# A third query block in two halves, and VectorE's share of the exponentials carried into the last block

## The chip, the cores and the metric

The kernel runs on one core of a Trainium2 chip. A core has five engines, each with an instruction queue of its own: TensorE (PE, matrix products into PSUM), VectorE (DVE), ScalarE (ACT, activation functions), GpSimd (POOL) and SyncE (SP, which here starts the DMAs). Each works through its queue in order and waits on semaphores where another engine's result or buffer is needed. The metric is the time of one launch on the device, in microseconds.

## What is computed

A transformer block of 2048 rows and 640 columns: layer norm, attention with 32 heads of 20 columns, output projection and residual; then layer norm, a gated layer with 1728 hidden columns, and residual. Weights and activations are bf16.

```python
def reference(A_x, A_wqkv, A_wo, B_x, B_w_gate, B_w_up, B_w_down):
    def _A_ref(x, wqkv, wo):
        ...
        scores = jnp.einsum("bhqd,bhkd->bhqk", q, k) * (Dh ** -0.5)
        p = _softmax(scores, axis=-1)
        o = jnp.einsum("bhqk,bhkd->bhqd", p, v)
        ...
    def _B_ref(x, w_gate, w_up, w_down):
        g = jnp.einsum("bsd,df->bsf", x, w_gate)
        u = jnp.einsum("bsd,df->bsf", x, w_up)
        return jnp.einsum("bsf,fd->bsd", g * u, w_down)
    x = A_x
    h = x + _A_ref(_layernorm(x, axis=-1), A_wqkv, A_wo)
    h2 = h + _B_ref(_layernorm(h, axis=-1), B_w_gate, B_w_up, B_w_down)
    return h2
```

## The kernel before

**Tiles.** The 32 heads form 8 groups of 4 (`NG`, `HPG`); a group's heads lie at 32-row slots, so the K=32 score matmuls of a group run side by side in different rows of the array. The 2048 query rows form 4 blocks of 512 (`QB`), the keys 16 tiles of 128 (`NT`). Scores stand transposed: keys on partitions, queries along the free dimension. A *segment* is one group of one query pass over all keys; the list `segs` (L303 to L311) fixes their order: block 0 (its first four groups in four key chunks, while the projections are still made), then pass "1" and pass "2" with whole blocks of 512 queries, then block 3: groups 0 and 1 whole (pass "3", `SPLIT_G` = 2), groups 2 to 7 first for the first 256 queries (pass "A") and then for the last 256 (pass "B"). Below, block means query block, counted from 0, so that the third block is block 2.

**A score tile.** The units of all segments are strung together and cut into 683 tiles of 1536 columns (`EW`, three PSUM banks; two such tiles exist). `emit_S` (L440) writes the score matmuls of a tile (L450) and then one exponential on ACT (L463) which makes the probabilities `E` in bf16; the softmax's maximum is replaced by a constant shift, and the sums come out of an extra column of ones in the values `vx`.

**A unit for VectorE.** For some tiles the last 512 columns are left to DVE. `x_takes` (L474) decides, `emit_x` (L480) writes the first pass, which reads the scores from PSUM (L488, `xv`), and queues four more: L498 (`xm`), L499 and L500 (`xt`), L493 (`xe`), which together build the bits of a bf16 exponential. ACT then does 1024 columns of that tile. The queued passes (`x_pieces`) are one queue, worked off front to back by `step_x` whenever the planner sees DVE free. In block 3 `x_takes` allows a unit only when no other work is waiting.

**Probabilities times values.** `emit_AV` (L588) takes the units whose probabilities are there in groups and accumulates them in the one bank `acc` (L619), 8 matmuls of 512 columns or 16 of 256. When a segment is full, DVE copies it to `asb` (L630), and it is normalised: by `norm` (L525), where the sums go to DRAM and back, are inverted and spread by six DMAs on SP, and POOL multiplies (L549, into `On`); or, for the segments in `FAST` (the last of a pass, on which an output projection waits), by `job_norm` (L574) with matmuls by an identity (`sums_to_rows`, L559 to L566; `rows_to_cols`, L571) and one DVE product (L582). POOL's multiplication for block b waits until the projection of block b-1 has read `On`: `("om", b - 1) in done` (L546).

**Jobs.** Between the score tiles TensorE does other work, in *jobs*: generators that yield after a matmul or at a place where the job may be left. The bank `mi` is their only accumulator. `run_job` (L429) continues a job as long as the planner's own clock (`at`, with constants such as `S_NS` and `EXP_NS`) shows room before ACT needs the next scores. `urgent` jobs go ahead of others (`step`, L365). Where there is no work, `keep_warm` (L424) puts in two filler matmuls that feed nothing (L427).

**The tail of a block.** When all groups of a block are normalised, `add_tail` (L975) queues: load the rows of x and the first weights, `job_out` (output projection and residual, L834 and L838; the layer norm's steps go to DVE's queue `aux`; then transposes, L260), `job_glu` (the gated layer, for 512 columns by `glu_sum`, L900, L247 and L908; for 256 by `glu_pair`, L918, L923 and L925; weights come in pairs of 256 hidden columns, the next pair is asked for when the one before starts, the last four pairs stay resident from the start of block 3), `job_y` (second matrix, L955, residual L959, result stored by SP, L965). So block 0's tail runs during pass "1", and so on; block 2's during block 3. Block 3's tail comes in two halves: rows 0 to 255 during pass "B", where the load and the projection are put into `urgent` if block 2's results are half out (`early`, L992), and the rest in `last_tail` (L1035) after the last exponential. One half row of the first half's `y` is held back (`some`, `held`) and placed in `last_tail`'s layer norm by `fill` (L1076).

**The loop** (L1125) goes through the tiles: scores and exponential, AV, events, a look whether a block is normalised, a job, fillers, spare DVE steps.

Of the kernel before, what the change touches and what calls it, by code (L numbers as in the profile page):

```python
# [57 lines left out]
X_LEAST, X_OUT = 3, 6  # L58
# [13 lines left out]
def kernel(  # L72
# [23 lines left out]
    ep = pool("ep", 6)  # L96
# [132 lines left out]
    def dve(ns):  # L229
        ready = at["pe"] + LAT  # L230
        spare(ready)
        at["dve"] = max(at["dve"], ready) + ns
# [69 lines left out]
    PASS = {"0": (0, 0, QB), "1": (1, 0, QB), "2": (2, 0, QB), "3": (3, 0, QB), "A": (3, 0, HW), "B": (3, HW, HW)}  # L302
# [6 lines left out]
    segs += [(p, g, 0, NT, "only") for p in "12" for g in range(NG)]  # L309
    segs += [("3", g, 0, NT, "only") for g in range(SPLIT_G)]  # L310
    segs += [(p, g, 0, NT, "only") for p in "AB" for g in range(SPLIT_G, NG)]  # L311
    FINAL = len(segs) - 1
    FAST = {("2", NG - 1), ("A", NG - 1), ("B", NG - 2)}
# [15 lines left out]
    x_pieces = deque()  # L329
    x_left = {}  # L330
    x_put = []
    x_live = {"units": 0}
    x_last = set()
# [7 lines left out]
    waiting = deque()  # L341
    aux = deque()
# [21 lines left out]

    def step():  # L365
        if cur["fresh"] and (urgent or waiting):
            if cur["gen"] is not None:
                jobs.appendleft((cur["key"], cur["gen"]))
            cur["key"], cur["gen"] = (urgent or waiting).popleft()
# [33 lines left out]
    def step_aux():  # L403
        while aux:
            try:
                at["dve"] += next(aux[0]) or 200
                return True
            except StopIteration:
                aux.popleft()
        return False  # L410

    def spare(until):
        while at["dve"] + (x_pieces[0][0] if x_pieces and not aux else 600) <= until + TOL:
# [8 lines left out]
    COST = {"T": 300, "v": 680}  # L422
# [6 lines left out]
    def run_job(until):  # L429
        if cur["fresh"]:  # L430
            key = urgent[0][0] if urgent else cur["key"] if cur["gen"] is not None else jobs[0][0] if jobs else None
            if not waiting and (key is None or max(at["pe"], at["mi"]) + SWITCH + COST.get(key[0], LEAST) > until):
# [7 lines left out]
    def emit_S(i):  # L440
# [14 lines left out]
        begin = max(at["pe"], at["slot"][-2])  # L455
        at["pe"] = begin + S_NS
# [17 lines left out]
    def x_takes(i):  # L474
        us, n = tiles[i]
        s = us[-1][0]
        return (n == EW and segs[s][4] == "only" and (PASS[segs[s][0]][0] < LAST_B or not jobs and not cur["gen"]) and last_tile[s] - i >= X_LEAST and len({u[0] for u in us}) == 1
                and len(x_pieces) < 3 and at["dve"] < at["pe"] + TOL and x_live["units"] < X_OUT)

    def emit_x(ps, us):  # L480
# [3 lines left out]
        m = xp.tile([P, BANK], I32, name="xm")  # L484
        t = xp.tile([P, BANK], F32, name="xt")
# [3 lines left out]
        x_live["units"] += 1  # L489
        x_left[s] = x_left.get(s, 0) + 1  # L490

        def last():
# [3 lines left out]
            x_last.update({(s, us[-1][1], us[-1][2])})  # L496
        x_pieces.extend([
# [3 lines left out]
            (700, last)])  # L501
# [19 lines left out]
    def need_x(s):  # L521
        while x_left.get(s):
            step_x()

    def norm(s, asb):  # L525
# [9 lines left out]
        def back():  # L535
# [9 lines left out]
            def mult():  # L545
                if b and ("om", b - 1) not in done:  # L546
# [7 lines left out]
    def sums_to_rows(asb, w):  # L554

        n = w // SLOT
        ps = bank()
        for t in range(w // P):
            nc.tensor.matmul(ps[:, HPG * t:HPG * (t + 1)], lhsT=asb[:, t * P:(t + 1) * P], rhs=identf[:, DH:P:SLOT], start=True, stop=True)  # L559
        r16 = sums_all[:, col["n"]:col["n"] + n]  # L560
# [27 lines left out]
    def emit_AV(upto):  # L588
# [6 lines left out]
        i, s = av_q[0][0:2]  # L595
        p, g, lo, hi, kind = segs[s]
        b, c0, w = PASS[p]
        if acc["seg"] != s:
            if at["pe"] < at["acc"] and now["i"] < acc["from"]:
# [10 lines left out]
        if ready < min(most, acc["left"]) and i > upto - 3:  # L610
            return
# [646 lines left out]
```

## Time and profile before

| | us |
|---|---|
| median of 3 runs (967.95 to 971.46) | 971.15 |
| the profiled execution | 968.8 |
| its span, first to last instruction | 966.9 |
| ScalarE busy, share of the span | 899.6, 93% |
| TensorE busy (matmuls) | 837.9, 87% |
| VectorE busy | 606.3, 63% |
| GpSimd busy | 61.6, 6% |
| mean granted TensorE clock | 0.976 |

A share says how much of the span an engine had an instruction in work; since the matmuls overlap and their ends are modelled, 87% of TensorE is not 87% of its peak. The costliest groups are the exponentials (683 for 882.3 us), the score matmuls (204.6 and 69.6 us) and the probability matmuls (169.5 us). The first exponential starts at 16.4 us, the last ends at 925.2; what lies behind is the last half tail.

The rows of the profile by slices of the span show where the engines thin out: VectorE's tenths fall in the last third, where it has no units.

```profile
PE   7778889888887898998898999988888899888897
PEld 5233333222232222331233223322332334444465
DVE  7664348888778778888878887878462231143243
ACT  6879999999999999999999999999799999899951
```

Each digit is the busy share of one of 40 equal slices in tenths.

### The profile page before, as it was taken

The page shows a single profiled execution, that of the slowest core. Times are in us where ns is not written, and L with a number is a line of the kernel's source. Part 1 is how long each engine was busy: PE and PEld are TensorE (multiplying, and loading weights), DVE is VectorE, ACT ScalarE, POOL GpSimd, SP SyncE. Part 2 cuts the span into 40 slices and gives each one's busy share as a digit, 9 for nine tenths or more (in the row PEclk, how much of TensorE's full clock was granted, in tenths as well). Part 3 has the DMA queues.
Part 4 walks back from the last instruction along what each step waited for, and adds up shares of the span by engine and source line. Part 5 has one row for each costly group of instructions (what it writes and reads, how often), then busy time and mean ns, then how long its engine had stood idle before and what let it go on. Part 6 is the DMA issues. An engine that isn't in the chain of part 4 may idle for free.

```text
span 966.9 us, 18074 instructions
## 1 busy us (share of the span) xinstructions
PE 837.9 (87%) x7176; PEld 328.5 (34%) x7257; DVE 606.3 (63%) x1224; ACT 899.6 (93%) x719; POOL 61.6 (6%) x155
## 2 busy tenths in 40 slices
PE   7778889888887898998898999988888899888897
PEld 5233333222232222331233223322332334444465
DVE  7664348888778778888878887878462231143243
ACT  6879999999999999999999999999799999899951
POOL 3120011000000000000000000000000000000000
PEclk9999999999999899997999999999799999899999
DMA  6000010010050131014021230103202001102310
GB/s 184 28 1 1 1 26 24 20 39 13 20 178 2 39 85 43 20 43 177 7 68 33 67 87 13 34 20 104 65 3 67 19 8 27 55 19 63 75 42 17
DMA packets 67819, 44.46 MB, mean 46 GB/s; under 512 B 18504, under 2 KB 63404, under 8 KB 67728
## 3 DMA queue, kind: packets, MB, share of 16 engines
q1 hardware_dynamic: 67728, 43.23, 16.0%
q8 instruction: 59, 0.97, 0.4%
q14 instruction: 32, 0.26, 0.1%
HBM read 35.91 MB, written 7.30 MB: 45 GB/s over the span
## 4 chain that ended last, share of the span: by engine, by line
ACT 40%; PE 35%; issue 14%; DVE 9%; DMA 1%; POOL 0%; SPq 0%; ACTq 0%; DVEq 0%; POOLq 0%
ACT E L463 40%; PE sc L450 9%; PE acc L619 6%; PE mi L278 4%; PE mi L900 3%; PE mi L955 3%; PE mi L834 2%; PE f L900 2%; PE mi L427 1%; PE mi L292 1%; PE f L955 1%; DVE kT L285 1%; DVE st L182 1%; PE mi L918 1%; DVE u L247 1%
## 5 line engine op out<-in xcount | busy, mean ns | idle before, releaser
L463 ACT ACTIVATE E<-sc 128x1536 bf16<-128x1536 f32 (+1 forms) x683 | 882.3, 1460 | 27.1 <-PE sc L450 22.0
L450 PE MATMUL sc<-qa,kT 32*128 32x512 bf16 x1536 | 204.6, 390 | 54.2 <-ACT E L463 43.4
L450 PEld LDWEIGHTS <-kT 32*128 32x128 bf16 x2432 | 84.5, 91 | 293.2 <-issue 254.5
L619 PE MATMUL acc<-E,vx 128*32 128x512 bf16 (+1 forms) x2330 | 169.5, 357 | 0.5 <-ACT E L463 0.5
L488 DVE TENSOR_SCALAR xv<-sc 128x512 f32<-128x512 f32 x102 | 70.3, 689 | 38.9 <-PE sc L450 38.2
L278 PE MATMUL mi<-lnT,wp 128*128 128x512 bf16 x284 | 79.5, 380 | 14.0 <-DVE qa L285 6.6
L450 PE MATMUL sc<-qb,kT 32*128 32x256 bf16 (+1 forms) x896 | 69.6, 294 | 14.7 <-ACT E L463 12.3
L549 POOL TENSOR_TENSOR on<-asb,bc 128x512 bf16<-128x512 f32 (+1 forms) x30 | 36.0, 1198 | 718.1 <-DMA bc<-scr 468.7
L500 DVE SCALAR_TENSOR_TENSOR xt<-xt,xm 128x512 f32<-128x512 f32 x102 | 74.0, 726 | 2.3
L493 DVE SCALAR_TENSOR_TENSOR xe<-xt,xv 128x512 int16<-128x512 f32 x102 | 74.0, 726 | 1.3
L499 DVE SCALAR_TENSOR_TENSOR xt<-xm 128x512 f32<-128x512 int32 x102 | 70.9, 695 | 2.2
L619 PEld LDWEIGHTS <-vx 128*32 128x32 bf16 x2432 | 44.4, 96 | 67.4 <-issue 67.2
L955 PE MATMUL mi<-wd,hh 128*128 128x320 bf16 x378 | 66.0, 301 | 0.3 <-DVE xr L959 0.3
L427 PE MATMUL mi<-kT,ident 128*128 128x512 bf16 x189 | 61.6, 397 | 4.0 <-DVE on L582 1.8
L900 PE MATMUL mi<-ln2T,wu 128*128 128x512 bf16 (+1 forms) x158 | 46.0, 387 | 6.0 <-DVE hh L908 5.4
L955 PEld LDWEIGHTS <-hh 128*128 128x128 bf16 x448 | 38.1, 97 | 38.1 <-issue 26.6
L247 DVE CAST u<-mi 128x512 bf16<-128x512 f32 (+1 forms) x42 | 28.9, 688 | 34.9 <-PE mi L900 33.3
L908 DVE TENSOR_TENSOR hh<-mi,u 128x512 bf16<-128x512 f32 (+1 forms) x42 | 28.8, 686 | 33.9 <-PE mi L900 31.3
L900 PE MATMUL mi<-ln2T,wg 128*128 128x512 bf16 (+1 forms) x160 | 44.7, 381 | 5.9 <-DVE u L247 5.3
L498 DVE TENSOR_SCALAR xm<-xv 128x512 int32<-128x512 int32 x102 | 44.7, 438 | 0.5
L278 PEld LDWEIGHTS <-wp 128*128 128x128 bf16 x310 | 25.9, 97 | 55.6 <-issue 39.5
L834 PE MATMUL mi<-wo,on 128*128 128x320 bf16 x224 | 38.4, 303 | 1.5 <-DVE xr L838 1.3
(150 smaller groups left out, 611.3 us busy)
## 6 DMA issues: line engine op xcount, KB each, us to landing
bc<-scr SPq DMA_DIRECT2D x100, 64.0 KB
wu<-in_B_w_up_dram SPq DMA_DIRECT2D x20, 320.0 KB
wg<-in_B_w_gate_dram SPq DMA_DIRECT2D x20, 320.0 KB
qsp<-qa SPq DMA_DIRECT2D x8, 384.0 KB
xr<-in_A_x_dram SPq DMA_DIRECT2D x16, 160.0 KB
out_dram<-xr SPq DMA_DIRECT2D x14, 160.0 KB
wd<-in_B_w_down_dram SPq DMA_DIRECT2D x13, 160.0 KB
xs<-in_A_x_dram SPq DMA_DIRECT2D x3, 640.0 KB
```

The source lines that it names most:

```text
L278: nc.tensor.matmul(ps[:], lhsT=wslice(m, g, c), rhs=lnT[:, c, ch * QB:(ch + 1) * QB], start=(c == 0), stop=(c == KT - 1))
L427: nc.tensor.matmul(ps[:], lhsT=ident[:], rhs=kT[0][:, 0:BANK], start=True, stop=True)
L450: nc.tensor.matmul(sc[:, o:o + w], lhsT=kT[g][SLOT * j:SLOT * (j + 1), kt * P:(kt + 1) * P], rhs=q_of(g, b, c0, w)[SLOT * j:SLOT * (j + 1) ...
L463: exps = nc.scalar.activation(e[:, 0:n_act], sc[:, 0:n_act], ACT.Exp, bias=EXP_BIAS, scale=SM_SCALE)
L488: took = nc.vector.tensor_scalar(v[:], ps, X_SCALE, X_BASE, ALU.mult, ALU.max)
L493: nc.vector.scalar_tensor_tensor(e[:], t[:], X_C, v[:], ALU.add, ALU.add)
L499: (700, lambda: nc.vector.scalar_tensor_tensor(t[:], m[:], X_A, m[:], ALU.mult, ALU.mult)),
L500: (700, lambda: nc.vector.scalar_tensor_tensor(t[:], t[:], X_B, m[:], ALU.add, ALU.mult)),
L619: nc.tensor.matmul(acc["t"][SLOT * j:SLOT * (j + 1), 0:w], lhsT=vx[kt][:, VS * h:VS * h + SLOT], rhs=e, start=(acc["n"][j] == 0), stop=(ac ...
L834: nc.tensor.matmul(ps[:, 0:HALF], lhsT=on[g][:, t * P:(t + 1) * P], rhs=wo[g][:, cs], start=(g == 0), stop=(g == NG - 1))
L900: nc.tensor.matmul(ps[0:M, 0:n], lhsT=st["w", fp][k][:, c, f2 * P:f2 * P + M], rhs=st["ln2T"][:, c, c0:c0 + n], start=(c == 0), stop=(c == ...
L955: nc.tensor.matmul(ps[:, 0:HALF], lhsT=st["hh"][f][0:K, t * P:(t + 1) * P], rhs=late["Wd"][f][0:K, cs], start=(f == 0), stop=(f == 2 * FP ...
```

## The change

Four things are done together.

1. Pass "2" is cut like pass "3": groups 0 and 1 whole, groups 2 to 7 as pass "C" (first 256 queries) and pass "D" (last 256). Block 2 then has two tails of 256 rows, queued when C and when D are normalised. `FAST` holds the last segment of each. The condition "block b-1 has been read" becomes `read_out`, which asks for all its tails (`TAILS`).
2. VectorE's units: in block 3 a unit is now taken where TensorE had to wait for a score buffer (`idle > X_IDLE`). Two units may be open at once, as chains whose passes are taken in turn (`next_x`), each with its own `xm` and `xt` buffers; five results may wait instead of six. Near a segment's end a unit needs more distance if more than two passes are queued.
3. Urgent jobs begin only once their input is there by the planner's clock (`opens`, `first`), `job_norm` yields its costs, and the `early` rule is gone. In the half tails from block 2 on, the rows of x are loaded when the tail is queued, outside the job.
4. `emit_AV` may run twice for a tile, and takes what it has when a probability buffer (`E_BUFS` = 6) is about to be needed again.

The constants of point 2 also hold in blocks 0 to 2. The core of the diff:

```diff
-X_LEAST, X_OUT = 3, 6
+X_IDLE, X_LEAST, X_OUT, X_DEP = 0, 3, 5, 90
+E_BUFS = 6
...
+    PASS = {"0": (0, 0, QB), "1": (1, 0, QB), "2": (2, 0, QB), "3": (3, 0, QB),
+            "C": (2, 0, HW), "D": (2, HW, HW), "A": (3, 0, HW), "B": (3, HW, HW)}
...
+    segs += [("1", g, 0, NT, "only") for g in range(NG)]
+    for full, halves in ("2", "CD"), ("3", "AB"):
+        segs += [(full, g, 0, NT, "only") for g in range(SPLIT_G)]
+        segs += [(p, g, 0, NT, "only") for p in halves for g in range(SPLIT_G, NG)]
     FINAL = len(segs) - 1
-    FAST = {("2", NG - 1), ("A", NG - 1), ("B", NG - 2)}
+    TAILS = {0: [0], 1: [0], 2: [0, 2]}
+    FAST = {("C", NG - 1), ("D", NG - 1), ("A", NG - 1), ("B", NG - 2)}
...
+    def first():
+        return urgent and (opens.get(urgent[0][0], 0) < at["pe"] + SWITCH or not (waiting or jobs or cur["gen"]))
+
     def step():
-        if cur["fresh"] and (urgent or waiting):
+        if cur["fresh"] and (first() or waiting):
...
-        if start == at["exp"] and x_takes(i):
+        if start == at["exp"] and x_takes(i, idle):
...
-        return (n == EW and segs[s][4] == "only" and (PASS[segs[s][0]][0] < LAST_B or not jobs and not cur["gen"]) and last_tile[s] - i >= X_LEAST and len({u[0] for u in us}) == 1
-                and len(x_pieces) < 3 and at["dve"] < at["pe"] + TOL and x_live["units"] < X_OUT)
+        return (n == EW and segs[s][4] == "only" and (PASS[segs[s][0]][0] < LAST_B or idle > X_IDLE) and last_tile[s] - i >= X_LEAST + (3 if sum(map(len, x_chains)) > 2 else 0) and len({u[0] for u in us}) == 1
+                and len(x_chains) < 2 and at["dve"] < at["pe"] + TOL and len(x_live) < X_OUT)
...
-        m = xp.tile([P, BANK], I32, name="xm")
-        t = xp.tile([P, BANK], F32, name="xt")
+        m = xp.tile([P, BANK], I32, name="xm", bufs=2)
+        t = xp.tile([P, BANK], F32, name="xt", bufs=2)
...
+    def next_x():
+        chain = next((c for c in x_chains if c is not x_prev["chain"]), x_chains[0])
+        return x_chains[0] if len(chain) == 1 else chain
+
     def step_x():
-        if not x_pieces:
+        if not x_chains:
             return False
-        ns, fn = x_pieces.popleft()
-        at["dve"] += ns
+        chain = next_x()
+        ns, fn = chain.popleft()
+        at["dve"] += ns - (X_DEP if chain is not x_prev["chain"] else 0)
...
+    def read_out(b):
+        return all(("om", b, t) in done for t in TAILS[b])
...
-        bc = sums_to_rows(asb, w)
-        yield NEXT
+        ps = sums_on_pe(asb, w)
+        yield 780 * w // QB
+        dve(700)
+        bc = sums_to_rows(ps, w)
         yield NEXT
         ps = rows_to_cols(bc, w, bank())
-        assert b == 0 or ("om", b - 1) in done
+        yield 1030 * w // QB
+        dve(690 * w // QB)
+        assert b == 0 or read_out(b - 1)
...
-        if ready < min(most, acc["left"]) and i > upto - 3:
+        if ready < min(most, acc["left"]) and min(u[0] for u in av_q) > upto - 3:
             return
...
             elif (p, g) in FAST:
+                opens["nf", p, g] = at["dve"] + LAT
                 urgent.append((("nf", p, g), job_norm(s, asb)))
...
-        early = b == LAST_B and ("y", b - 1, 0) in done and ("y", b - 1, 1) not in done
-        if early:
-            urgent.append((("load",) + key, once(ready)))
-        else:
-            do(("load",) + key, ready)
+        if made:
+            rows()
+        do(("load",) + key, ready)
...
+    due = [("0", range(NG), 0, [0, 1, 2, 3]), ("1", range(NG), 1, [0, 1, 2, 3]), ("C", range(SPLIT_G, NG), 2, [0, 1]),
+           ("D", range(SPLIT_G, NG), 2, [2, 3]), ("A", range(SPLIT_G, NG), 3, [0, 1])]
...
-        emit_AV(i if i >= n_tiles else i - 2 if i >= LAG else i - 4)
+        for _ in range(2):
+            emit_AV(i if i >= n_tiles else i - 2 if i >= LAG else i - 4)
+            if not av_q or min(u[0] for u in av_q) > i - E_BUFS + 1:
+                break
...
-        if b_seen < NB - 1 and normed(str(b_seen), range(NG)):
-            add_tail(b_seen, list(range(TPB)))
-            b_seen += 1
-        if not a_seen and normed("3", range(SPLIT_G)) and normed("A", range(SPLIT_G, NG)):
-            add_tail(LAST_B, [0, 1])
-            a_seen = True
+        while due and normed(*due[0][0:2]) and (len(due[0][1]) == NG or normed(str(due[0][2]), range(SPLIT_G))):
+            add_tail(*due.pop(0)[2:])
```

In the new program the halves of block 2 are 768 score matmuls of 256 columns in place of 384 of 512.

More of the change, by code (lines that the diff above doesn't have):

```diff
@@ L598, in emit_AV @@
         if acc["seg"] != s:
-            if at["pe"] < at["acc"] and now["i"] < acc["from"]:
+            if at["pe"] < at["acc"] and now["i"] < acc["from"] and min(u[0] for u in av_q) > now["i"] - E_BUFS:
                 return
@@ L978, in add_tail, with rows @@
         key = (b, ts[0])
-        def ready():
+        made = b and (ts[0] or all(("y", b - 1, t) in done for t in (0, 2)))
+        def rows():
             if b not in tail_st:
```

79 lines of the change are left out of this document (42 added, 37 removed).

## The prediction

> **What bounds the kernel now.** I read the stages first (busy time of each engine in windows), cut where the first exponential of a block or pass runs: 16.4 to 249.8 query block 0, to 469.9 block 1, to 682.3 block 2, then block 3 as two whole groups (to 745.2), first halves A (to 832.9) and last halves B (to 925.2), and the end.
>
> ```profile
> core 0: us, PE busy (x) PEld busy (x) DVE busy (x) ACT busy (x) POOL busy (x), PEclk, DMA share, GB/s
> 249.80:469.90 220.10, 193.16 (x1431) 62.32 (x1441) 175.02 (x325) 214.61 (x173) 11.92 (x8) 0.95 0.22 67
> 469.90:682.30 212.40, 188.52 (x1445) 63.77 (x1463) 168.33 (x315) 212.09 (x172) 10.49 (x8) 1.00 0.19 50
> 682.30:745.20 62.90, 52.74 (x405) 20.77 (x409) 28.54 (x84) 57.88 (x45) 1.26 (x1) 0.92 0.18 50
> 745.20:832.90 87.70, 80.99 (x976) 35.37 (x985) 23.13 (x43) 87.09 (x64) 4.89 (x6) 1.00 0.11 28
> 832.90:925.20 92.30, 77.39 (x1026) 40.72 (x1032) 26.22 (x80) 87.10 (x65) 2.90 (x4) 0.96 0.18 45
> 925.20:966.90 41.70, 34.15 (x275) 25.43 (x274) 16.55 (x49) 9.93 (x24) 0.00 (x0) 0.99 0.11 30
> ```
>
> ScalarE (ACT) fills its stages: it idles 0.3 us of block 2's 212.4, while VectorE (DVE) is busy 168.3 of it. Block 3 has as many exponentials and takes 242.9 us; ACT idles 5.0, 0.6 and 5.2 us in its parts, and DVE has worked 77.9 us. So a column taken from ACT is time saved as long as TensorE (PE) delivers scores. The groups by form give a unit's price:
>
> ```profile
> L463 ACT ACTIVATE E<-sc 128x1536 bf16<-128x1536 f32 x580 | 803.5, 1524 | 24.4 <-PE sc L450 19.6 <-PE acc L619 3.5
> L463 ACT ACTIVATE E<-sc 128x1024 bf16<-128x1024 f32 x103 | 113.6, 1103 | 2.8 <-PE sc L450 2.4
> L488 DVE TENSOR_SCALAR xv<-sc 128x512 f32<-128x512 f32 x102 | 70.3, 689 | 38.9 <-PE sc L450 38.2
> L918 PE MATMUL mi<-ln2T,qa 128*128 128x256 bf16 x70 | 9.7, 274 | 1.1 <-DVE hh L925 1.1
> ```
>
> A tile that gives 512 columns to DVE costs ACT 1524 - 1103 = 421 ns less. Next, where ACT waits: the timeline of ACT at the turn from block 2 to 3, and the windows in which PE had half its clock.
>
> ```profile
> 687.67 2.79 ACT L463 ACTIVATE E<-sc 128x1536 bf16<-128x1536 f32 x2 [1.81 <-PE sc L450]
> 692.50 1.45 ACT L463 ACTIVATE E<-sc 128x1536 bf16<-128x1536 f32 x1 [2.03 <-PE sc L450]
> 694.98 5.48 ACT L463 ACTIVATE E<-sc 128x1536 bf16<-128x1536 f32 x4 [1.03 <-PE sc L450]
> ...
> 310.40:320.60 10.20, 8.67 (x52) 2.00 (x51) 6.13 (x12) 6.76 (x6) 0.00 (x0) 0.50 0.01 2
> 436.70:446.90 10.20, 8.87 (x51) 1.53 (x51) 6.69 (x12) 9.92 (x8) 0.00 (x0) 0.50 0.74 278
> 685.80:696.10 10.30, 9.14 (x49) 3.82 (x49) 5.16 (x10) 5.43 (x5) 0.00 (x0) 0.50 0.17 48
> 836.00:842.80 6.80, 5.93 (x45) 2.38 (x45) 0.42 (x1) 4.58 (x4) 0.00 (x0) 0.50 0.00 0
> ```
>
> The turn costs 1.81 + 2.03 + 1.03 = 4.87 us of ACT. PE stood in order behind the normalisation of the last group (L559, L571, L582), its clock fell to 0.50, and scores came late. Window less ACT busy, the four cold stretches idle ACT 3.44, 0.28, 4.87 and 2.22 us.
>
> **The change, part by part** (counts are from the order of instructions in the two built programs).
>
> Units. 127 instead of 102: 21, 42, 38 and 26 in blocks 0 to 3, where there were 19, 41, 40 and 2. 25 x 0.421 = -10.5 us of ACT. All but one net go to block 3. Their DVE work is 25 x (689 + 438 + 695 + 726 + 726) ns = 81.9 us, hidden there: block 3 leaves DVE 242.9 - 77.9 = 165 us. PE must deliver sooner by 10 us there. It can: the second layer of block 2, done in A until now, goes half into D and the first whole groups, so that A's other work on PE falls from 112 matmuls of L900 (0.214 us apart) and 112 of L955 (0.133 apart), 38.9 us, to 140 half ones (0.118) and 72 of 320 columns, 26.1 us. B's stays as it is, with PE busy 77.4 of 92.3 us. One bound is the full 10.5; the other is -8.8, if the 4 units added in the denser whole groups buy nothing. I take -10.5.
>
> Halves of block 2. Six score matmuls of 256 columns take 0.40 us where three of 512 take 0.39; sixteen acc matmuls of 256 take 0.62 us, as eight of 512 do: nothing on PE. The second layer's L900 groups become L918 groups: 10 matmuls of 256 run in about 1.18 us where 5 of 512 run in 1.07, so 28 x (1.18 - 1.07) = +3.1 us of PE; its evacuations go from 14 x (689 + 686) to 28 x (425 + 424) ns, +4.5 us of DVE. Both hide under ACT (PE idles 23.9 us of block 2 and 31.8 of block 3); with that cover gone PE's 3.1 would show.
>
> The turn from block 2 to 3. Its fast normalisation is 256 wide instead of 512 (4 pieces of L559 for 0.61 us instead of 8 for 1.56) and is no longer begun before its accumulator is copied (`opens`), and the residual rows are loaded before the job that needs them. Of 4.87 us I take back 2.4, half; the same rule for A's end at 837 to 846 us (0.38 + 1.78 + 0.47 + 0.22 = 2.85 us) gives 0.6. Bounds: 0 and -7.7. I take -3.0.
>
> What is added there. One more such end (C's), at most a B-like 2.85 us, at least 0: I take +1.5. The two half layers each start on a 256-wide first weight pair with the next pair just asked for. At 871 to 876 us such a start made ACT idle 1.14 + 0.34 = 1.48 us, since SP, in order, had held the weight loads behind the sums' round trip (sums at 866.21, sums_all at 867.83, wu at 868.21). SP gets 43 more DMAs: 20 bc, 15 of the other three steps, 8 weights. Behind a late weight load stand PE's next scores. Twice 1.48 is the upper bound, 0 the lower: +1.5.
>
> Earlier blocks. At the end of group 1 of block 1, forced DVE passes left PE without work and ACT idled 1.53 + 0.99 + 0.92 = 3.44 us. The new rules take no unit near a group's end when passes are queued, and pull probability matmuls before their buffer is needed; the thin PE slots stay. Between 0 and -3.4: -1.0.
>
> Passes in turn. DVE idles 2 us in all ahead of each kind of pass, and DVE isn't the bound: 0 on the path.
>
> The end. After the last exponential PE has 16 acc matmuls and 8 of `wd,hh` before the out projection, where it had 6 and 4: 0.2 + 4 x 0.133 = +0.75 us. Then two half rows of y (28 matmuls) stand in the layer norm's gap instead of one:
>
> ```profile
> 932.03 2.17 PE L955 MATMUL f<-wd,hh 128*128 128x320 bf16 x14
> 934.98 0.28 PE L260 MATMUL mi<-ident,ln 128*128 128x128 bf16 x2 [0.79 <-DVE ln L1074]
> ```
>
> 14 x 0.133 = 1.87 us more (the first 14 are issued by 934.05), of which 0.93 fit before 934.98: +0.94. Together +1.7.
>
> Sum: -10.5 - 3.0 + 1.5 + 1.5 - 1.0 + 1.7 = -9.8 us; the span goes from 966.9 to 957.1. The profiled run took 968.8 (1.9 around the span) and the median of the runs is 971.15, so I forecast 971.15 - 9.8 = 961.
>
> **The clock, by row and by rule.** 78 of the 216 filler matmuls (L427) go. Cold stretches followed windows of 3.4 us in which PE was busy 0.98, 1.40, 1.97 and 2.25 us; after others with 2.02 (904.3), 2.12 and 2.20 us the clock stayed full. So a thin window may or may not cost a stretch. The Trainium skill ("TensorE: Matmul & The Clock Gate", Part 1) has the clock halved after at least one idle window of about 3.4 us and given back after a busy one. No window here was idle for that long, yet four were punished, so the trace doesn't agree with idle in the strict sense. By the rule so read the rival below would have no chance at all; I keep it.
>
> **Rivals.**
> 1. Everything at the turns mends: both ends' 7.7 us go and 2 of the 3.44, nothing new comes but 0.0 to 0.7: -10.5 - 7.7 - 2 + 0.5 + 1.7 = -18, 953 us. For it: the waits come from order, which the change rewrites. Against: PE still has thin slots there, and the clock answers to those.
> 2. The cover is gone: the 3.1 us of PE show, both starts cost 1.48, the new end 2.85, nothing mends: -10.5 + 3.1 + 3.0 + 2.85 + 1.7 = +0.1, 971 us, no change. For it: PE is busy 0.89 of block 2. Against: ACT idles 0.3 us there at just that density.
> 3. The clock: thin slots after the first out projection in D, at the turn, in A's first group and in B's first two, with less filler, each drop PE to half for some 10 us with 4.87 us of ACT lost, as at 686: four more give 961.35 + 19.5 = 981 us, slower. It decides from three such stretches on (14.6 us). For it: 78 fillers fewer, and 0.98 to 2.25 us windows have dropped. Against: fillers go mostly where real work stands now, and windows at 2.02 to 2.20 passed.
> That the units do not come is excluded by the order.
>
> **How the numbers follow.** Forecast 0.60, rival 1 0.21, rival 2 0.12, rival 3 0.07. Faster by over 0.5% (under 966.3; half a per cent is about what a measurement of this kernel can tell from no change) are the first two: 0.81; same 0.12; slower 0.07. The bounds of the sum are -19.9 (951) and about -1.3 (970); 952 to 968 leaves out rivals 2 and 3.
>
> **What would show it.** 127 units, exponentials of 1024 columns in A and B; ACT busy 10 us less; the span from 682 to the last exponential down from 242.9 by 10 to 14 us with DVE near 150 us in it; ACT's waits at the turn under 3 us. Wrong if new gaps <-PE sc of more than 6 us stand in D or A, if PEclk 0.50 covers more than the 37.5 us of now, or if the end grows past 44.5 us.

## The result: 1.3% slower, and the profile after

| | before | after |
|---|---|---|
| median, us | 969.61 (4 runs, 967.95 to 971.46) | 981.51 (4 runs, 979.93 to 984.3) |
| ratio, 95% interval | | 1.0134 (1.0105 to 1.0163) |
| span of the profiled execution | 966.9 | 979.6 |
| ScalarE busy | 899.6 | 892.4 |
| VectorE busy | 606.3 | 675.6 |
| TensorE at half clock, all stretches (the prediction's 37.5 are the four longest) | 47.5 | 61.6 |

The windows by stage of the kernel after: first exponential of block 0, 1 and 2, then the whole groups of block 3, A, B and the end.

```profile
core 0: us, PE busy (x) PEld busy (x) DVE busy (x) ACT busy (x) POOL busy (x), PEclk, DMA share, GB/s
15.50:252.60 237.10, 200.78 (x1516) 70.20 (x1517) 158.88 (x301) 223.20 (x172) 21.79 (x67) 0.99 0.07 17
252.60:476.40 223.80, 196.11 (x1449) 61.62 (x1448) 176.07 (x333) 214.61 (x173) 11.05 (x8) 0.95 0.22 66
476.40:702.50 226.10, 200.58 (x2263) 84.36 (x2262) 169.64 (x359) 215.54 (x171) 10.43 (x12) 0.96 0.18 47
702.50:763.60 61.10, 52.17 (x444) 22.67 (x443) 32.19 (x64) 56.10 (x43) 0.72 (x1) 0.97 0.30 80
763.60:852.70 89.10, 76.94 (x1003) 38.30 (x1001) 50.13 (x114) 84.12 (x66) 7.05 (x7) 0.96 0.13 35
852.70:935.40 82.70, 73.03 (x1002) 38.70 (x1002) 59.92 (x137) 81.31 (x65) 3.20 (x5) 0.98 0.20 53
935.40:979.60 44.20, 36.78 (x295) 27.30 (x294) 16.95 (x50) 9.97 (x25) 0.00 (x0) 0.98 0.11 32
```

Take each row's length from its counterpart of before. Block 0 is 3.7 us longer, block 1 3.7, block 2 13.7; block 3, the next three rows together, has 232.9 against 242.9 and is 10.0 us shorter; the end is 2.5 longer, and the first exponential comes 0.9 sooner. The sum is the +12.7 of the spans. In block 2 ACT is busy 215.5 of 226.1 us where it was 212.1 of 212.4: it now waits ten microseconds in the block where it had hardly waited. The expected gain is there, in block 3; more than that was lost ahead of it, 21.1 us. The largest single piece stands in D (612.7 to 702.5): it takes 89.80 us, of which ACT is busy 81.17, while three eighths of block 2 before (a half pass of six of its eight groups) are 79.7 us.

The groups by form of the kernel after, busy time, mean, and idle time ahead with its releasers:

```profile
L476 ACT ACTIVATE E<-sc 128x1536 bf16<-128x1536 f32 x555 | 768.8, 1500 | 37.6 <-PE sc L462 27.0 <-PE acc L650 8.2
L476 ACT ACTIVATE E<-sc 128x1024 bf16<-128x1024 f32 x128 | 134.2, 1070 | 8.1 <-PE sc L462 5.9 <-PE acc L650 1.8
L501 DVE TENSOR_SCALAR xv<-sc 128x512 f32<-128x512 f32 x127 | 87.0, 687 | 48.9 <-PE sc L462 47.9
```

The 127 units are there, at 430 ns of ACT each (1500 - 1070). What ACT waits has grown from 27.2 to 45.7 us, and the part that the accumulator's matmuls end from 3.5 to about 10. Four of the six windows at half clock that stand in new places (the others are 6.8 us at 786.9 and 3.4 us at 926.9), and ACT's timeline at the turn from block 2 to 3:

```profile
210.04:213.44 3.40, 3.40 (x16) 0.63 (x15) 1.81 (x3) 1.44 (x2) 0.00 (x0) 0.50 0.24 74
623.00:633.20 10.20, 9.76 (x81) 4.28 (x81) 6.09 (x13) 8.44 (x7) 0.00 (x0) 0.50 0.04 12
664.00:670.80 6.80, 6.47 (x46) 2.35 (x46) 4.27 (x9) 2.89 (x3) 0.00 (x0) 0.50 0.35 93
708.40:711.80 3.40, 3.40 (x18) 1.60 (x17) 1.27 (x3) 2.76 (x2) 0.00 (x0) 0.50 1.17 298
```

```profile
702.54 2.79 ACT L476 ACTIVATE E<-sc 128x1536 bf16<-128x1536 f32 x2 [0.32 <-PE sc L462]
708.37 2.79 ACT L476 ACTIVATE E<-sc 128x1536 bf16<-128x1536 f32 x2 [3.04 <-PE sc L462]
712.61 2.79 ACT L476 ACTIVATE E<-sc 128x1536 bf16<-128x1536 f32 x2 [1.45 <-PE sc L462]
```

So the turn waits 0.32 + 3.04 + 1.45 = 4.81 us where it waited 4.87. What is late is another thing now: the weights.

```profile
700.15 3.00 SPq L567 DMA_DIRECT2D bc<-scr  x4
703.25 0.39 SPq L912 DMA_DIRECT2D wu<-in_B_w_up_dram  x1
706.46 0.72 PE L950 MATMUL mi<-ln2T,wu 128*128 128x256 bf16 x5 [2.61 <-DMA wu<-in_B_w_up_dram]
```

SP's and PE's rows of the same timeline: four DMAs of a normalisation hold SP for 3.0 us, the next weight pair is asked for only behind them, and PE, whose next scores stand behind its matmuls, waits 2.61 us for it.

Three readings of the trace went into the experiments. First, D: the first half tail's residual rows.

```profile
661.36 0.90 SPq L851 DMA_DIRECT2D xr<-in_A_x_dram  x2
...
663.79 0.49 DVE L868 TENSOR_TENSOR xr<-mi,xr 128x320 bf16<-128x320 f32 x1 [3.31 <-DMA xr<-in_A_x_dram]
...
664.33 1.49 PE L864 MATMUL mi<-wo,on 128*128 128x320 bf16 x5 [2.61 <-DVE xr L868]
...
666.49 2.48 ACT L476 ACTIVATE E<-sc 128x1536 bf16<-128x1536 f32 x2 [3.27 <-PE sc L462]
```

This timeline is read from top to bottom as a chain: the rows are asked for at 661.36, behind a sum's round trip, after the projection that needs them has begun; VectorE waits 3.31 us for them, in order, TensorE 2.61 us for its one accumulator bank `mi`, ScalarE 3.27 us for the scores behind; from 664.0 the clock is halved for 6.8 us.

Second, passes in turn: the end of a group in block 1.

```profile
312.14 0.68 DVE L511 SCALAR_TENSOR_TENSOR xt<-xm 128x512 f32<-128x512 int32 x1
312.74 0.42 DVE L510 TENSOR_SCALAR xm<-xv 128x512 int32<-128x512 int32 x1
313.07 0.68 DVE L512 SCALAR_TENSOR_TENSOR xt<-xt,xm 128x512 f32<-128x512 f32 x1
313.68 0.68 DVE L511 SCALAR_TENSOR_TENSOR xt<-xm 128x512 f32<-128x512 int32 x1
314.28 0.68 DVE L506 SCALAR_TENSOR_TENSOR xe<-xt,xv 128x512 int16<-128x512 f32 x1
...
315.01 0.38 PE L650 MATMUL acc<-xe,vx 128*32 128x512 bf16 x1 [0.42 <-DVE xe L506]
...
316.24 1.05 PE L650 MATMUL acc<-E,vx 128*32 128x512 bf16 x8 [0.85 <-DVE asb L661]
...
316.95 2.79 ACT L476 ACTIVATE E<-sc 128x1536 bf16<-128x1536 f32 x2 [2.80 <-PE acc L650]
```

The older unit's passes (L511, L512, L506) have the younger one's (L510, L511) between them. Its result `xe` is the last that the group needs: until it is there the accumulator can't be closed and copied, the next group's matmuls can't start, and they hold the probability buffer that ACT wants. ACT waits 2.80 us. Not all of this lateness is the turn: between the older unit's passes VectorE also makes two copies of `ln2T` and waits 0.79 us for TensorE.

Third, block 0: at 204.02 the sums of a group go out on SP behind 32 loads of `wo` (11.91 us from 192.01), VectorE's reciprocal waits 3.00 us for them, TensorE 3.04 us for the evacuation of q queued behind it, ACT 2.65 us; then come the 3.4 us at half clock at 210.04. Before has the same loads ahead, but its sums go out 2.2 us sooner and its reciprocal waits only 0.90 us for them.

### The profile page after: what moved, and what is told of

Read it like the earlier page. It is cut to its first block, busy times and chain, and to the rows that moved or that the text cites. A ratio compares the mean times of both kernels' runs of the same rounds, so it can differ in the third digit from the quotient of the medians.

```text
span 979.6 us, 20113 instructions
## 1 busy us (share of the span) xinstructions
PE 847.4 (87%) x8087; PEld 352.6 (36%) x8087; DVE 675.6 (69%) x1392; ACT 892.4 (91%) x719; POOL 61.8 (6%) x160
## 4 chain that ended last, share of the span: by engine, by line
PE 37%; ACT 33%; DVE 13%; issue 13%; DMA 2%; POOL 1%; SPq 0%; ACTq 0%; DVEq 0%; POOLq 0%
ACT E L476 33%; PE sc L462 9%; PE acc L650 7%; PE mi L950 4%; PE mi L932 4%; PE mi L987 3%; PE mi L280 3%; PE mi L438 2%; PE f L932 2%; PE f L987 1%; DVE xe L506 1%; DVE hh L957 1%; DVE u L955 1%; PE mi L864 1%; DVE xt L511 1%
## 5 line engine op out<-in xcount | busy, mean ns | idle before, releaser
L462 PE MATMUL sc<-qa,kT 32*128 32x512 bf16 (+1 forms) x1920 | 207.8, 348 | 47.3 <-ACT E L476 37.6
L650 PE MATMUL acc<-E,vx 128*32 128x256 bf16 (+1 forms) x2640 | 177.4, 336 | 4.2 <-DVE asb L661 3.9
L501 DVE TENSOR_SCALAR xv<-sc 128x512 f32<-128x512 f32 x127 | 87.0, 687 | 48.9 <-PE sc L462 47.9
L506 DVE SCALAR_TENSOR_TENSOR xe<-xt,xv 128x512 int16<-128x512 f32 x127 | 90.6, 714 | 1.1
L512 DVE SCALAR_TENSOR_TENSOR xt<-xt,xm 128x512 f32<-128x512 f32 x127 | 88.5, 699 | 1.1
L511 DVE SCALAR_TENSOR_TENSOR xt<-xm 128x512 f32<-128x512 int32 x127 | 88.2, 700 | 1.0
L573 POOL TENSOR_TENSOR on<-asb,bc 128x256 bf16<-128x256 f32 (+1 forms) x35 | 36.5, 1044 | 729.0 <-DMA bc<-scr 574.5
L987 PE MATMUL mi<-wd,hh 128*128 128x320 bf16 x364 | 65.6, 308 | 2.1 <-DVE xr L991 2.0
L510 DVE TENSOR_SCALAR xm<-xv 128x512 int32<-128x512 int32 x127 | 56.7, 452 | 0.9
L987 PEld LDWEIGHTS <-hh 128*128 128x128 bf16 x448 | 39.5, 98 | 39.4 <-issue 26.7
L955 DVE CAST u<-mi 128x256 bf16<-128x256 f32 (+1 forms) x42 | 17.7, 422 | 44.9 <-PE mi L950 44.7
L864 PE MATMUL mi<-wo,on 128*128 128x320 bf16 x224 | 41.4, 311 | 4.2 <-DVE xr L868 4.1
L438 PE MATMUL mi<-kT,ident 128*128 128x512 bf16 x138 | 43.3, 397 | 1.9 <-DVE hh L957 0.6
L650 PE MATMUL acc<-xe,vx 128*32 128x256 bf16 (+1 forms) x176 | 44.2, 338 | 0.4 <-DVE xe L506 0.4
```

The source lines that it names most:

```text
L438: nc.tensor.matmul(ps[:], lhsT=ident[:], rhs=kT[0][:, 0:BANK], start=True, stop=True)
L462: nc.tensor.matmul(sc[:, o:o + w], lhsT=kT[g][SLOT * j:SLOT * (j + 1), kt * P:(kt + 1) * P], rhs=q_of(g, b, c0, w)[SLOT * j:SLOT * (j + 1) ...
L501: took = nc.vector.tensor_scalar(v[:], ps, X_SCALE, X_BASE, ALU.mult, ALU.max)
L506: nc.vector.scalar_tensor_tensor(e[:], t[:], X_C, v[:], ALU.add, ALU.add)
L510: (480, lambda: nc.vector.tensor_scalar(m[:], v[:].bitcast(I32), 0x7FFF, 0x8000, ALU.bitwise_and, ALU.bitwise_or)),
L511: (700, lambda: nc.vector.scalar_tensor_tensor(t[:], m[:], X_A, m[:], ALU.mult, ALU.mult)),
```

## The experiments

In the expectations, theory L is "inputs come late at the half tails, behind SP's queue", T "passes in turn end the older unit late", U "the units themselves cost", C "the clock, whatever is late", P "the chance of the clock", E "TensorE's leftover work sets the end". Each ratio is against the kernel before, on the same chip, with its 95% interval; two variants are best compared by their ratios, since not all of them ran on one chip (0.001 is about 1 us). Lengths by block are from the profiles, cut at the same exponentials as the windows above.

### e1: the halves without the new rule for units

```diff
-X_IDLE, X_LEAST, X_OUT, X_DEP = 0, 3, 5, 90
+X_IDLE, X_LEAST, X_OUT, X_DEP = 0, 3, 6, 0
...
-        ... (PASS[segs[s][0]][0] < LAST_B or idle > X_IDLE) ...
+        ... (PASS[segs[s][0]][0] < LAST_B or not jobs and not cur["gen"]) ...
...
-        chain = next((c for c in x_chains if c is not x_prev["chain"]), x_chains[0])
-        return x_chains[0] if len(chain) == 1 else chain
+        return x_chains[0]
```

> The halves of block 2 and the new job rules, with the old rule for VectorE's units (98 units, 5 of them in block 3, passes in one queue). Theory L (late inputs: the half tails of block 2 wait for rows of x and for weights behind SP's queue, and the cold clock lengthens it): slower than before by 8 to 20 us, 977 to 990 us, with the ACT waits of 2 us and more in D's second part and at the start of pass 3 still there. Theory U (the units themselves cost the time, by passes that end late): 965 to 972 us, those waits gone.

977.34 us, 1.0107 (1.0075 to 1.0139). The halves and the new rules of order, with 98 units, are slower than before without any new unit. The time lies at the lower edge of L's range, but the waits that L named aren't there: VectorE waits for no rows of x in D, and ScalarE's longest waits in D and at the start of pass 3 are 1.85 and 0.67 us. Nor is all of it at the half tails: block 0 alone is 7.9 us longer in its profile, block 2 8.4, block 3 5.9 shorter. Its block 0 has the same late sums behind the loads of `wo` (3.06 us of VectorE, and 3.19 of ScalarE behind it), so this wait doesn't need passes in turn.

### e2: no units in block 3

```diff
-        ... (PASS[segs[s][0]][0] < LAST_B or idle > X_IDLE) ...
+        ... PASS[segs[s][0]][0] < LAST_B ...
```

> The changed kernel with no unit in block 3 (101 units instead of 127), all else by the same rules. Theory L: 26 units fewer cost ScalarE 26 x 0.421 = 10.9 us, so slower than the changed kernel by 5 to 11 us, 987 to 992 us. Theory U: the waits in block 3 go with the units, at or below the changed kernel's 981.5 us, 972 to 982 us.

989.64 us, 1.0255 (1.0212 to 1.0299), 8.1 us over after by the medians and some 12 by the ratios. By the profiles block 3 is 8.7 us longer than after's, while the end is 2.8 shorter. Units in the last block pay: that the units of block 3 themselves cost the time, as U had it here, is out.

### e3: the passes in order of arrival

```diff
-        chain = next((c for c in x_chains if c is not x_prev["chain"]), x_chains[0])
-        return x_chains[0] if len(chain) == 1 else chain
+        return x_chains[0]
```

(and `X_DEP` 0; 120 units.)

> The changed kernel with VectorE's passes in order of arrival instead of in turn (120 units). Theory L: within 4 us of the changed kernel, 978 to 986 us; the waits of ScalarE on the probability matmuls at the ends of groups (9.9 us in five places) may shrink, those for DMAs stay. Theory U: 968 to 975 us, since passes in turn finish the older unit of two up to three passes later.

970.31 us, 1.003 (1.0006 to 1.0054): the expectation of L is missed, and U's range is hit, by the reason that it gave here, the turn, which is T from now on. One rule, which the prediction had at nothing, is worth 10 us (1.0134 less 1.003), although 7 units fewer leave ScalarE 3 us more work. The same place of block 1 in its timeline:

```profile
309.06 0.69 DVE L511 SCALAR_TENSOR_TENSOR xt<-xm 128x512 f32<-128x512 int32 x1
309.78 0.69 DVE L512 SCALAR_TENSOR_TENSOR xt<-xt,xm 128x512 f32<-128x512 f32 x1
310.51 0.69 DVE L506 SCALAR_TENSOR_TENSOR xe<-xt,xv 128x512 int16<-128x512 f32 x1
...
313.36 2.00 ACT L476 ACTIVATE E<-sc 128x1024 bf16<-128x1024 f32 x2 [0.87 <-PE acc L649]
```

Here the unit's passes follow each other, 1.45 us from L511 to L506 where after takes 2.14, and ACT's wait there is 0.87 us instead of 2.80. The loads of `wo` also fall differently (12, then the sums, then 20), and the wait of block 0 is gone. Block 0 is 1.8 us shorter than after's, block 1 5.0, block 2 1.9, block 3 3.6; the end is 1.9 longer.

### e4: the kernel before, with units in block 3

```diff
-        ... (PASS[segs[s][0]][0] < LAST_B or not jobs and not cur["gen"]) ...
+        ... (PASS[segs[s][0]][0] < LAST_B or idle > 0) ...
```

> The kernel before with one rule changed: in block 3 a unit is taken where TensorE had to wait for a score buffer (123 units, 23 of them in block 3, where there were 2). Theory L: the units pay, 21 x 0.421 = 8.8 us of ScalarE less, of which the end gives back up to 5 us (three half rows of y more stand after the last exponential): 960 to 968 us. Theory U: no gain or slower, 969 to 978 us.

967.54 us, 1.0003 (0.9983 to 1.0024): no change, at the edge of what L expected. 123 units; the last exponential ends 9.2 us sooner (916.0), but 56 matmuls of the second matrix (L956, `wd,hh`) for block 3's first half stand behind the last score matmul instead of 22, and the end takes 46.7 us instead of 41.7. The profiled execution, the second fastest of ten, gains 4.2 us, the median nothing.

### e5: the rows of x asked for one job earlier

```diff
-            if not made:
+            if not made and not placed:
                 rows()
...
+        placed = [k for k, j in enumerate(jobs) if j[0] == ("y", b - 1, 2)] if b == 2 and not made else []
...
+        if placed:
+            jobs.insert(placed[0], (("rows",) + key, once(rows)))
```

> The changed kernel with the rows of x for block 2's first half tail asked for one job earlier (before the last two rows of block 1's second layer instead of right before the projection that adds them). Theory L: ScalarE's waits of 3.27 + 1.42 us at 666 to 670 us go and a stretch of half clock with them: 4 to 8 us faster than the changed kernel's 981.5, 973 to 978 us. Rival C (the thin work of TensorE at that turn and the half clock cost the time whatever is late): 979 to 984 us.

975.38 us, 1.009 (1.0065 to 1.0114): as L had it, 4.3 us under after by the ratios (6.1 by the medians). VectorE no longer waits for the rows, and D's row of the windows is 81.60 us with the clock at 1.00:

```profile
615.00:696.60 81.60, 72.32 (x986) 35.88 (x987) 61.62 (x136) 81.24 (x65) 3.66 (x5) 1.00 0.18 47
```

After had 89.80 us here, at 0.90. Both of D's half-clock stretches are gone, the earlier one at 623 too, which the rows can't have caused; the order around it moved with the edit. So the gain isn't the rows' alone: in after ScalarE waits 3.27 + 1.42 us behind the rows and 0.30 + 1.08 + 0.97 us in the stretch at 623.

### e6: the second weight pair asked for with the first

```diff
+            load_w(1, tail_st[b])
...
-                load_w(1, tail_st[b])
```

> The changed kernel with the second pair of weights of every tail asked for together with the first, before the projection; the order of work on TensorE is the same. Theory L: ScalarE's waits of 0.76 + 0.32 us at 700 us go, and those of 3.04 + 1.45 us at 708 to 713 us at least by half, since the third pair can be asked for one pair earlier only if its buffer is free: 975 to 979 us. Rival C: 979 to 984 us.

985.7 us, 1.0181 (1.0153 to 1.021): no gain, if anything 4 us slower than after; a miss for L. The edit doesn't reach what was late: the pair awaited at 706 us is asked for when the pair before it starts, and TensorE's wait for it stayed at 2.84 us. So the price of the late weights isn't shown by this run.

### e7: the kernel before, with passes in turn

The `next_x`, the two chains, `X_OUT` 5, the distance rule and the rules of `emit_AV` of the change, put into the kernel before; whole blocks and the old rule for block 3.

```diff
+    def next_x():
+        chain = next((c for c in x_chains if c is not x_prev["chain"]), x_chains[0])
+        return x_chains[0] if len(chain) == 1 else chain
...
+        for _ in range(2):
+            emit_AV(i if i >= n_tiles else i - 2 if i >= LAG else i - 4)
```

> The kernel before with VectorE's units as two chains in turn (108 units: 21, 42, 43 and 2 in the blocks), blocks whole, block 3 with the old rule, and with the new rules for the probability matmuls. Theory T (passes in turn end the older unit late, so that groups close late and ScalarE waits for probability buffers, in blocks 0 to 2 too): slower than before, 970 to 978 us, with waits of ScalarE on the probability matmuls of 6 us and more. Rival P (the 7 us that the changed kernel lost in blocks 0 and 1 are where the clock happened to fall): 963 to 969 us, those waits near the 3.5 us of before.

976.78 us, 1.0091 (1.0073 to 1.011): T holds. ACT's waits in the view of waits: e7's, after's, and the accumulator's line of before and of e3:

```profile
ACT E L467 <- PE sc L454: 26.0, 32, 3.9
...
ACT E L467 <- PE acc L632: 8.8, 5, 3.0
```

```profile
ACT E L476 <- PE sc L462: 32.9, 40, 4.2
...
ACT E L476 <- PE acc L650: 9.9, 5, 2.8
```

```profile
ACT E L463 <- PE acc L619: 3.5, 3, 1.7
```

```profile
ACT E L476 <- PE acc L649: 7.9, 5, 2.0
```

The columns are us in total, times and the longest. Five waits for the accumulator, 8.8 us, without any half block; before has 3.5 us in three. By blocks e7 differs from before by +4.2, +5.2, +1.3 and -1.9 us. The other new rules of this edit are in e3 too, whose blocks 0 and 1 stand at +1.9 and -1.4 to before; so it is the turn. How it costs is seen best in block 1: ScalarE waits 4.6 us for the accumulator there in after, 4.8 in e7, 1.7 in before and 0.9 in e3. In the whole kernel e3 still has 7.9 us of such waits, two of them (1.99 and 1.82 us) in block 2. In the other blocks the price of the turn is shown by the two swaps, and its path isn't traced.

### e8: order of arrival, rows and weights early

The edits of e3, e5 and e6 together, 122 units.

> The changed kernel with passes in order of arrival, the rows of x one job earlier and the second pair of weights with the first (122 units). Theory L and T together: the 970.3 us of the kernel with passes in order less the DMA waits in D and at the turn (4.7 and 3 to 5.6 us): 958 to 964 us, faster than before. Rival C: 968 to 973 us.

967.28 us, 0.9993 (0.9977 to 1.0009): the gains over after add up (13.7 us by the ratios, where e3 has 10.1 and e5 4.3), to the time of before and not below, a miss of 3 us. That the sum fits is in part chance: in e3 VectorE waits only 0.73 us for the rows of x, so what e8 gains over e3 isn't the wait that e5 removed. Against the profile of before, block 2 is 8.0 us longer, block 3 13.8 shorter, the end 4.6 longer.

### e9: order of arrival, block 2 whole

```diff
-    for full, halves in ("2", "CD"), ("3", "AB"):
+    segs += [("2", g, 0, NT, "only") for g in range(NG)]
+    for full, halves in (("3", "AB"),):
...
-        chain = next((c for c in x_chains if c is not x_prev["chain"]), x_chains[0])
-        return x_chains[0] if len(chain) == 1 else chain
+        return x_chains[0]
```

(and `X_DEP` 0, the lists of tails and of fast normalisations for a whole block 2, and a line that makes sure the last rows are loaded.)

> The kernel after with pass 2 whole again (no C and D, one tail for block 2) and the passes in order of arrival, as in e3; all else new (units in block 3, the new rules for AV and urgent jobs); 122 units. If the halves of block 2 and the passes in turn are together the whole of what was lost (theories L and T), the kernel before with the units of block 3 in it: blocks 0 and 1 as in e3 (loss 17 and 9 us), block 2 near 4 us of loss instead of 12.5, block 3 near 230 us, end some 46 us: 958 to 963 us. If the new rules for AV and urgent jobs cost too, or TensorE's work is what block 3 and the end now share, no better than e4: 966 to 970 us.

979.02 us, 1.0083 (1.0054 to 1.0112): worse than either expectation, and the most telling run. It has 129 units, not the 122 of the expectation. Its exponentials end at 907.3 us, 17.9 sooner than before's; then comes an end of 70.1 us. Rows of TensorE's timeline behind the last exponential, and the window of the half clock in it:

```profile
910.70 1.25 PE L950 MATMUL mi<-ln2T,qa 128*128 128x256 bf16 x10 [0.97 <-DVE hh L957]
915.15 2.29 PE L950 MATMUL mi<-ln2T,qa 128*128 128x256 bf16 x10 [0.97 <-DVE hh L957]
918.41 2.29 PE L950 MATMUL mi<-ln2T,qa 128*128 128x256 bf16 x10 [0.97 <-DVE hh L957]
...
937.01 8.50 PE L987 MATMUL f<-wd,hh 128*128 128x320 bf16 x56
```

```profile
911.80:915.20 3.40, 1.46 (x13) 1.02 (x11) 1.70 (x4) 0.00 (x0) 0.00 (x0) 1.00 0.00 0
915.20:932.30 17.10, 13.20 (x58) 8.22 (x58) 4.24 (x10) 0.00 (x0) 0.00 (x0) 0.50 0.00 1
```

The gated layer of block 3's first half isn't done when ScalarE is: 80 of its matmuls of 256 (L950) and all 56 of L987 are left. With nothing between them each ten wait 0.97 us until VectorE has emptied the one bank `mi`, and 50 of the 80 run at half clock. In after nothing of L950 is left, nor in e3, which differs from e9 by the halves and what follows from them. That is what halving block 2 is good for: its second layer is out of the way sooner, and more of the last block's work on TensorE fits under the exponentials. The same pair of runs gives the price: block 2 takes 8.8 us longer in halves (224.3 us in e3, 215.5 in e9). ScalarE waits 5.0 us more in it, and VectorE takes 34 units there instead of 41, 2.9 us at the forecast's price.

### e10: later DMAs of a normalisation asked by GpSimd

```diff
-            nc.sync.dma_start(scr[:]...)
+            nc.gpsimd.dma_start(scr[:]...)
...
-                nc.sync.dma_start(bc[SLOT * j:SLOT * (j + 1), 0:w], ...)
+                nc.gpsimd.dma_start(bc[SLOT * j:SLOT * (j + 1), 0:w], ...)
```

(on e8)

> e8 with five of the seven DMAs of each slow normalisation (scr from ri, and the four that spread it into bc) asked by GpSimd instead of SyncE, so that weights and rows no longer stand behind them in SP's queue; same order of work on TensorE, ScalarE and VectorE. If loads late behind SP's queue are what is left (theory L), ScalarE's waits at the start of each gated half layer go (3 to 5 us in blocks 2 and 3): 961 to 965 us. If they are not, or GpSimd's issuing takes as long as it saves, 966 to 972 us.

965.36 us, 0.9963 (0.9945 to 0.9981): 0.3% better against before than e8, but not by the path expected. TensorE's waits for the second weight pair at 689 us are 1.00 + 0.39 us where e8 has 1.15 + 0.45. The profiled execution is no faster than e8's. Inconclusive.

### e11: the kernel before, units in block 3 except in B

```diff
-        ... (PASS[segs[s][0]][0] < LAST_B or not jobs and not cur["gen"]) ...
+        ... (PASS[segs[s][0]][0] < LAST_B or idle > 0 and segs[s][0] != "B") ...
```

> The kernel before with units in block 3 where TensorE had to wait, as in e4, but none in its last pass (B): 115 units instead of 123. Theory E (TensorE's leftover work sets the end: e9's exponentials ended 18 us earlier than those of before and its end took 28 us longer): 13 units more than before take 5.5 us from ScalarE, and 42 half-layer matmuls of the second matrix are left behind the last exponential instead of 22, 2.7 us: 964 to 968 us, about 3 us under before, and no slower than e4 although it has 8 units less. If the units of pass B were worth their 0.42 us each, 3 us over e4: 970 to 972 us.

965.2 us, 0.9967 (0.995 to 0.9984): theory E holds. With 8 units less than e4 it is no slower; the exponentials end 3.3 us later (919.3) and the end is 2.7 shorter (44.0). It is faster than both kernels, by 0.3% than before and, by the medians, 1.7% than after.

### e12: e11 with GpSimd's DMAs

e10's edit on e11.

> e11 with the five later DMAs of each slow normalisation asked by GpSimd instead of SyncE, as in e10, so that weight loads do not stand behind them in SP's queue. Theory L: the waits at the start of the gated half layer of pass B (1.5 us in before) and some of the turn go, as e10 stood 3 us better to before than e8: 962 to 966 us, and under before. If before's waits at the turn come of the order on TensorE alone, as e11: 964 to 968 us.

969.77 us, 1.0017 (0.9996 to 1.0038): a miss for both expectations, and 0.5% slower than e11. In block 3 of e11 no matmul waits for weights, so there was nothing to gain, and each of the 170 DMAs now takes GpSimd 0.5 to 0.6 us ahead of its multiplications. That makes e10's small gain no proof for L either.

## Why the prediction was wrong

By its own steps, and against what the runs showed:

| step of the prediction | forecast, us | shown |
|---|---|---|
| "Units." | -10.5 | block 3 is 10.0 us shorter by the windows, pass A's end (below) included; in e2, without them, it is 8.7 longer than in after |
| "Halves of block 2." | 0 | block 2 +13.7; halves against a whole block, with the passes in order, 8.8 (e3 and e9) |
| "The turn from block 2 to 3." | -3.0 | nothing back at the turn, 4.87 us of waits before and 4.81 after; at A's end all 2.85 us are gone (no wait from 848.7 to 873.5) |
| "What is added there." | +1.5 and +1.5 | ScalarE waits 2.4 us at C's end (629 to 634), 4.7 behind the late rows, 0.8 at 700, and the turn's 4.8 now for weights |
| "Earlier blocks." | -1.0 | +7.4; +0.5 without the turn (e3) |
| "Passes in turn." | 0 | +9 (e7), 10 back when undone (e3); most of "Earlier blocks" is in it |
| "The end." | +1.7 | +2.5 |

The rows overlap and don't add up to the 12.7 us. Two steps failed outright, and a third was priced too low. **"DVE idles 2 us in all ahead of each kind of pass, and DVE isn't the bound: 0 on the path"** counted VectorE's throughput. The cost is not throughput but the time at which one particular result is there: a unit's last pass closes a group, and the copy, the next group and the probability buffers queue behind it. Taking turns saves VectorE 0.12 us per pass (starts 0.60 us apart in after, 0.72 in e3), which nobody needed, and puts 0.7 us into the chain that a group's end waits for. The prediction asked what an operation costs and not who waits for its last one, though it had named that place itself ("forced DVE passes left PE without work"). So the term "Earlier blocks" had the wrong sign: the rules that it counted on are in e3 as well as in after, and in e3 the two blocks together are 0.5 us longer than in before, in after 7.4.

**"the residual rows are loaded before the job that needs them"** was false in D, in the section on the change too. The diff loads them at queueing only if the block before has been put out (`if made`), and block 1's last `y` hadn't been. The prediction read the branch that suited. The rows were then asked for inside the job, behind other DMAs: 3.31 us of VectorE, 3.27 of ScalarE, and the clock. That belongs to "What is added there", which had a B-like end as its upper bound, 2.85 us; ScalarE's waits behind the rows are 3.27 + 1.42 us, and e5, which moved a stretch at half clock too, is 4.3 us faster than after by the ratios. The lateness belongs to the order in which after is planned, not to the halves as such: in e1 VectorE waits for no rows in D, in e3 0.73 us.

**"Halves of block 2"** had 0, by the engines' work alone: "Both hide under ACT". Between e3 and e9 the halves cost block 2 8.8 us, of which 5.0 are waits of ScalarE and 2.9 the units that VectorE no longer takes there. Which rule keeps it from taking them wasn't tried.

With the turn and the late rows undone (e3 and e5 with e6, that is e8) the time is that of before: 0.7 us under it by the ratio, where 9.8 were forecast. The rest is in the end and block 2: in block 2 ScalarE waits 4.9 us more than before, and e8 has 35 units where before has 40, which is 2.1 us; and it has 56 matmuls of the second matrix behind the last score where before has 22. "The end" was reckoned from after's own order and is right in size; but it is the place to which the gain goes when the exponentials are made faster. The profiled ends line up with that count: 41.4 to 41.9 us with 22 (before, e2, e7), 43.1 with 36 (e1), 43.4 to 44.2 with 42 (after, e6, e11, e12), 45.9 to 46.9 with 56 (e3, e4, e5, e8, e10). Of the 9.2 us by which e4's exponentials end sooner, its end takes back 5.0.

**The number of rival 3 came true, its mechanism at most in part.** It gave 981 us by four more stretches at half clock, which lose 19.5 us. There are 14.1 us more at half clock, and four of the six stretches in new places begin during or right behind a wait of ScalarE (the sums at 209, the rows at 664, the weights at 706, the accumulator at 786). The other two don't. Up to 628.7 ScalarE had not waited for 20 us; the clock fell at 623.0, behind a window of 3.4 us with TensorE busy 2.66, and then ScalarE waited 0.30 + 1.08 + 0.97 us for scores. In the stretch at 926.9 it waited 0.89 us. So where the clock came first, 3.2 us of waits followed, and the rival needs 19.5. e5 removed a late input, and both stretches of D are gone; e3 removed the turn, and the half-clock time fell to 52.3 us. e6 has most, 74.2 us, and is only 4 us slower than after. By how much the half clock lengthens the other waits isn't shown. So it was by luck that the rival's 981 us met the time.

Of the signs that the prediction named for itself, the 127 units, block 3 (10.0 us shorter) and the end (44.2 us) came; ACT is busy 7.2 us less where 10 were expected, and two signs of being wrong came too: 61.6 us at half clock, and over 7 us of ScalarE's waits for scores in D.

What stays open: the price of the weights of the third pair (e6 and e12 missed them; asking for them still earlier wasn't tried), what the half clock costs by itself, which rule takes units from a halved block 2, and why e1's block 0 is 7.9 us longer: 3.2 of it are the wait behind the late sums.

## What to carry over

Before an engine with idle time is given reordered work, find the one result in it that others wait for, and price its lateness, not the engine's load. Work taken from the bounding engine near the end of a kernel is worth less, and can be worth nothing, once the next engine's backlog sets the end: count what stands behind the last instruction of the bound, some 0.15 us for each matmul here ((46.7 - 41.7) / 34 in e4). A load that is "made early" is early only in the branch taken; look in the order of the queue, at what it stands behind.

## What was not expected of the hardware

**The half clock can hold.** In e9's end TensorE was busy 13.2 of 17.1 us, 77%, and the clock stayed at 0.50 all that time. For the first 13.7 us it ran in an even beat of 2.29 us of matmuls and 0.97 us of waiting, which leaves it busy 2.4 of every 3.4 us; the last 3.4 us were filled, and behind them the clock rose. The window before the drop had 1.46 of 3.4 us. The Trainium skill ("TensorE: Matmul & The Clock Gate", Part 1) gives the clock back after a busy window of about 3.4 us: the rise agrees, and the hold does if such a window with 0.97 us of waiting in every 3.27 isn't counted as busy.

**A chain of dependent VectorE passes costs little more than a mixed one**: 0.72 us from start to start (e3, 309.06 to 309.78) against 0.60 (after, 313.68 to 314.28), for passes of 512 columns.
